# Ten blocks of experts: the second gate's logits of the first halves on three other engines

## The chip, the cores and the metric

The kernel runs on one core of a Trainium2 chip. The metric is the device time of one execution in microseconds (us). The engines are TensorE (PE; PEld is its weight load), VectorE (DVE), ScalarE (ACT), GpSimd (POOL) and SyncE (SP), each with an instruction queue of its own that it works off in order.

## What is computed

Attention with rotary positions over 4 x 8 heads, and then two layers of experts on the 2304 tokens of 512 numbers that come out. The cut shows the two layers.

```python
def _moe_ref(x, modality_id, w_gate, modality_bias, w1, w2):
    logits = x @ w_gate + modality_bias[modality_id]
    e_idx = np.argmax(logits, axis=1)
    ...                                    # gate_w: softmax probability of e_idx
    for e in range(E):                     # E = 8, w1 512 x 1024, w2 1024 x 512
        mask = e_idx == e
        h = np.maximum(x[mask] @ w1[e], 0.0)
        out[mask] = gate_w[mask, None] * (h @ w2[e])

def _moe2_ref(x, w_skip, w_gate, w1, w2):
    do_compute = x @ w_skip > 0
    out = x.copy()
    xc = x[do_compute]
    ...                                    # the same routing and experts on xc: y
    out[do_compute] = xc + y
```

With the inputs as they are drawn, 2171 tokens of the first layer go to one expert and 133 to another. Of its 2304 outputs 716 pass the skip test of the second layer: 487, 123, 93, 6, 4, 2 and 1 of them go to seven experts.

## The kernel before

The instructions of every engine are written in program order by hand, and no planner moves them. Attention fills about the first 350 us. In its tail the tokens are sorted by expert into a list in DRAM (list0), and the first block of the first expert layer is begun.

The first layer (moe1) works on blocks of 256 tokens of one expert. body(i) does block i: mm1 in four phases g, each followed by ACT's relu (m_hi) and DVE's remainder (m_lo), which together write hT as a high and a low part; then mm2 on the first 128 tokens (half 0) and on the second (half 1), each into a psum tile y of two buffers (psY). Between the two halves xt(i + 1) transposes the tokens of the next block. fetch gathers tokens from DRAM with POOL, seq_load loads an expert's weights with SP if the expert changes, and seq_split divides them into two parts on ACT and DVE (w1s, w2s). Blocks 0 to 8 are certain; from 9 on every body stands in a conditional of its own (nest, L1292). With these inputs there are ten blocks, and only the tenth has a new expert.

A half's epilogue, epi(i, t, stage), routes its tokens for the second layer while the blocks go on:

- stage 0: ACT scales y by the gate weight into x2; three small POOL operations prepare the token index.
- stage 1: PE turns x2 with four transposes into psT, ACT copies them out, and POOL scatters x2 to out in DRAM.
- stage 2: PE multiplies x2t by the nine columns of gate and skip weights (wg2s): the logits. DVE chooses the expert (one-hot oh) in eight small operations, ACT does the exponential.
- stage 3: PE counts with oh and with acc2, the running count of tokens per expert.
- stage 4: DVE works out the place in the second list and adds oh to acc2, and POOL scatters token and weight to list1.

Half 0's stages all lie in body(i), between the pieces of mm2 on half 1. Half 1's stages 1 to 4 lie behind the four phases of mm1 in body(i + 1), and those of the last block in the first block of the second layer.

The second layer (moe2) works on blocks of 128 tokens, ten here. It adds its result to out with a gather and a scatter per block. At the end of body(6) moe2_ahead takes the counts so far, picks the leading expert and fixes its first two blocks. Two pairs of raw weight tiles are used in turn: (raw1, raw2) and (raw1b, raw2b). Before the change the leading expert's weights are loaded into (raw1b, raw2b) in body(7) by ACT's queue, and those of the next expert into (raw1, raw2) in the last body by SP's.

Of the kernel before, what the change touches and what calls it, by code (L numbers as in the profile page):

```python
# [10 lines left out]
F32 = mybir.dt.float32  # L11
F32R = mybir.dt.float32r
BF16 = mybir.dt.bfloat16
I32 = mybir.dt.int32
AF = mybir.ActivationFunctionType
ALU = mybir.AluOpType
# [96 lines left out]
class Kernel:  # L113
# [6 lines left out]
    def run(self):  # L120
# [3 lines left out]
        self.lists = [dp.tile([NLIST, 2], F32, name=f"list{i}") for i in range(2)]  # L124
        self.ident = cp.tile([128, 128], F32, name="ident")
# [18 lines left out]
        with ExitStack() as s:  # L144
            self.wp = s.enter_context(tc.tile_pool(name="moe", bufs=1, reuse_waits="tile"))
            self.pp = s.enter_context(tc.tile_pool(name="mps", bufs=1, space=PSUM, reuse_waits="tile"))
            self.bank = lambda name: self.rot("ps" + name, [128, 512], psum=True)
            self.moe_tiles()
            self.moe1()
            self.moe2()  # L150
# [818 lines left out]
    def moe_tiles(self):  # L969
        wp = self.wp  # L970

        self.slots2 = [(self.raw1, self.raw2), (wp.tile([128, 4, F], F32, name="raw1b"), wp.tile([128, 8, DM], F32, name="raw2b"))]
        self.xh = [wp.tile([128, DM], F32, name=f"xh{i}") for i in range(2)] + [self.xh2]
        for t in self.xh:
            self.nc.gpsimd.memset(t, 0.0)
        self.xT2 = wp.tile([128, 2, 4, B2], F32R, name="xT2")
        self.slots["xT"] = [[self.xT0, wp.tile([128, 2, 4, B1], F32R, name="xT1")], 1]

# [132 lines left out]
    def moe1(self):  # L1111
# [12 lines left out]
        def xt(i, h):  # L1124
            if i >= q.n:
                return
            if h == 0:
                xts[i] = self.rot("xT", [128, 2, 4, B1], F32R)
            self.transposed(xts[i], self.xg[i % 2][:, h, :], h * 128)
# [19 lines left out]
        def epi(i, t, stage):  # L1149
            s = eps[i, t]  # L1150

            def tl_(name, shape, dt=F32):
                return self.rot("e_" + name, shape, dt)

            if stage == 0:

                l = q.ls[i][0]
                x2 = s["x2"] = self.rot(f"x2{t}", [128, DM], bufs=1)
                s["ti"] = self.rot(f"ti{t}", [128, 1], I32, bufs=1)
                s["v"] = self.rot(f"ev{t}", [128, 3], bufs=1)  # L1160
                s["tg"] = self.rot(f"tg{t}", [128, 2], bufs=1)
                nc.scalar.activation(x2, s["y"], AF.Copy, scale=l[:, t, 1:2])
                nc.gpsimd.tensor_copy(s["ti"], l[:, t, 0:1])
                nc.gpsimd.tensor_scalar(s["v"][:, 0:1], l[:, t, 0:1], float(N), None, op0=ALU.is_lt)
                nc.gpsimd.tensor_copy(s["tg"][:, 0:1], l[:, t, 0:1])
            elif stage == 1:
# [7 lines left out]
            elif stage == 2:  # L1174
                v = s["v"]
# [3 lines left out]
                lg, nm, d = tl_("lg", [128, E + 1]), tl_("nm", [128, 1]), tl_("d", [128, E])  # L1179
                nc.vector.tensor_copy(lg, pg[:, 0 : E + 1])  # L1180
# [7 lines left out]
                nc.vector.tensor_reduce(m8, t8, axis=AX.X, op=ALU.max)  # L1188
                nc.vector.tensor_scalar(v[:, 1:2], lg[:, E : E + 1], 0.0, v[:, 0:1], op0=ALU.is_gt, op1=ALU.mult)
# [3 lines left out]
            elif stage == 3:  # L1193
# [3 lines left out]
            else:  # L1197
                v, oh = s["v"], s["oh"]
                nc.vector.tensor_scalar(s["se"], s["se"], 1e-9, None, op0=ALU.add)
                nc.vector.reciprocal(s["tg"][:, 1:2], s["se"])  # L1200
# [7 lines left out]
                self.scatter(self.lists[1], si, s["tg"], E * CAP)  # L1208
# [5 lines left out]
        def body(i):  # L1214
            def load2(c):
                if i == sure - 2:
                    self.moe2_load(1, c)

            more = None if i < sure - 1 else self.n1 > i + 1 - NA1
            if more is not None:  # L1220

                with tc.If(self.n1_sp > i + 1 - NA1) as cmp:
                    pass
                with cmp.Else():
                    self.moe2_second()
# [9 lines left out]
            for g in range(4 if i else 0):  # L1235
                mm1(i, g)
                if i == sure - 2:
                    self.moe2_load(0, g)
                epi(i - 1, 1, g + 1)
# [9 lines left out]
            mm2(i, 0, range(0, 8))  # L1249
            epi(i, 0, 0)  # L1250
            xt(i + 1, 0)
            xt(i + 1, 1)
            mm2(i, 1, range(0, 2))
            epi(i, 0, 1)
            load2(0)
            mm2(i, 1, range(2, 4))
            epi(i, 0, 2)
# [12 lines left out]
            epi(i, 0, 3)  # L1270
            epi(i, 0, 4)
            epi(i, 1, 0)
# [23 lines left out]
        self.last = dict(eps[sure - 1, 1])  # L1296
        nest(sure)
        eps[-1, 1] = self.last
# [36 lines left out]

    def moe2_second(self):
        q = self.q2
        for i in range(2):
            self.load(q.slots[0][i], q.w[i], self.reg(self.e2, [ET.SP], E - 1))
# [4 lines left out]
    def moe2(self):  # L1344
# [14 lines left out]
        def body(i):  # L1359
# [30 lines left out]
            def last(stage):  # L1390

                if i == 0:
                    self.epi(-1, 1, stage)

            def split1(pieces):
                self.seq_split(q, i + 1, 0, pieces)
# [13 lines left out]

            if i == 0:
                split2(0, range(0, 4))
            mm1(0, range(0, 2))
            last(1)
# [5 lines left out]
            last(2)  # L1420
            mm1(1, range(0, 2))
            split1((0,))
            h_tr(0)
# [3 lines left out]
            last(3)  # L1427
# [5 lines left out]
            last(4)  # L1433
# [96 lines left out]
```

## Time and profile before

| | |
|---|---|
| median of 3 runs | 760.42 us (759.24 to 762.78) |
| the profiled execution | 761.6 us, its span 760.0 us |
| busy in the span: PE, PEld | 718.9 us (95%), 652.8 us (86%) |
| busy in the span: DVE, ACT, POOL | 504.1, 441.8, 360.6 us |
| granted TensorE clock, mean | 0.979 of full speed |

The span runs from the first to the last instruction of the profiled execution; times in the rows further down count from its start. A matmul's end is modelled, so the step from one row's start to the next is the safer length. Attention takes about 0 to 354 us, the first layer's blocks to 609 us, the second layer the rest.

### The profile page before, as it was taken

What the parts mean: (1) busy time and instruction counts of PE and PEld (TensorE: products, weight loads), DVE (VectorE), ACT (ScalarE), POOL (GpSimd) and SP (SyncE); (2) the same over time, 40 slices, a digit from 0 to 9 for tenths busy, and PEclk for the clock granted to TensorE, in tenths of its full rate; (3) what the DMA queues carried; (4) which work ended last, traced back from release to release, by engine and by line L of the source; (5) the groups of instructions that cost most, each with busy time, mean ns of one, the idle gap of its engine ahead of it and who ended that gap; (6) DMA issues with size and microseconds to landing.
All of it is one profiled execution on the core that took longest, in us unless ns stands there. A gap on an engine that the chain in (4) does not pass through costs nothing. (4 is left out here: it accounts for less than half of the span.)

```text
span 760.0 us, 15381 instructions
## 1 busy us (share of the span) xinstructions
PE 718.9 (95%) x4948; PEld 652.8 (86%) x4948; DVE 504.1 (66%) x1216; ACT 441.8 (58%) x940; POOL 360.6 (47%) x497
## 2 busy tenths in 40 slices
PE   6899999999999999979999999999999969999994
PEld 6799999999999999878889988998998858877773
DVE  6789999999999999972533323333437643489892
ACT  3788888888888888861222222222235432388781
POOL 7655576868686863344433231332435412132232
PEclk8899999999999999999999999999999989999997
DMA  5665555555656554560011101110785201679900
GB/s 139 134 156 135 136 132 140 129 129 135 161 115 145 137 118 87 136 191 1 14 58 46 54 31 41 43 42 29 235 293 171 95 6 40 245 251 332 335 26 20
DMA packets 75341, 92.30 MB, mean 121 GB/s; under 512 B 29582, under 2 KB 50318, under 8 KB 75232
## 3 DMA queue, kind: packets, MB, share of 16 engines
q1 hardware_dynamic: 66080, 73.75, 35.6%
q0 software_dynamic: 7200, 12.46, 5.3%
q10 hardware_dynamic: 1952, 4.85, 2.0%
q8 instruction: 43, 0.70, 0.4%
q14 instruction: 66, 0.54, 0.3%
HBM read 62.12 MB, written 12.95 MB: 99 GB/s over the span
## 5 line engine op out<-in xcount | busy, mean ns | idle before, releaser
L428 PE MATMUL S<-w1s 128*128 128x288 f32 x640 | 134.1, 323 | 4.0 <-ACT w1s L384 1.3
L1145 PE MATMUL psY<-w2s,hT 128*128 128x512 f32 x480 | 119.4, 397 | 0.0
L1096 PE MATMUL psM<-xT,w1s 128*128 128x256 f32 x864 | 110.9, 285 | 0.0
L428 PEld LDWEIGHTS S<-w1s 128*128 128x128 f32 x640 | 98.7, 192 | 8.8 <-ACT PP L445 1.7
L1096 PEld LDWEIGHTS psM<-xT,w1s 128*128 128x128 f32 x864 | 105.2, 189 | 0.6 <-issue 0.6
L1145 PEld LDWEIGHTS psY<-w2s,hT 128*128 128x128 f32 x480 | 87.2, 188 | 16.8
L445 ACT ACTIVATE PP<-S,nm 128x576 f32<-128x576 f32 x128 | 95.9, 749 | 6.5 <-DVE nm L441 4.4
L441 DVE TENSOR_REDUCE nm<-S 128x1 f32<-128x576 f32 x128 | 94.9, 751 | 3.8 <-PE S L428 3.7
L530 DVE TENSOR_TENSOR tl<-T,th 128x512 fp32r<-128x512 f32 x128 | 88.0, 688 | 12.6 <-ACT th L526 9.3
L523 PE MATMUL T<-ident,PP 128*128 128x128 f32 x512 | 94.3, 274 | 0.8 <-DVE w1s L397 0.4
L526 ACT CAST th<-T 128x512 fp32r<-128x512 f32 x128 | 75.2, 587 | 17.6 <-PE T L523 15.1
L557 PE MATMUL O<-th,vh 128*128 128x288 f32 x256 | 76.4, 331 | 0.9 <-ACT os L566 0.9
L1109 DVE SCALAR_TENSOR_TENSOR hT<-psM,hT 128x512 fp32r<-128x512 f32 x36 | 24.9, 691 | 65.8 <-ACT hT L1104 53.7
L1369 PE MATMUL psM<-w1s,xT 128*128 128x512 f32 x240 | 62.0, 406 | 6.3 <-DVEq L1292 6.3
L523 PEld LDWEIGHTS T<-ident,PP 128*128 128x128 f32 x512 | 63.9, 140 | 3.4 <-DVE tl L530 1.0
L1409 PE MATMUL psY<-w2s,hT 128*128 128x512 f32 x240 | 63.7, 403 | 2.7 <-DVE hT L1388 2.7
L557 PE MATMUL O<-tl,vh 128*128 128x288 f32 x256 | 64.4, 305 | 0.0
L1104 ACT ACTIVATE hT<-psM 128x512 fp32r<-128x512 f32 x36 | 21.5, 598 | 70.6 <-PE psM L1096 70.1
L960 POOL DMA_INDIRECT list<-tg,si x20 | 20.2, 1009 | 88.7 <-issue 56.6
L1369 PEld LDWEIGHTS psM<-w1s,xT 128*128 128x128 f32 x240 | 44.7, 192 | 16.5 <-issue 6.4
L328 POOL TENSOR_TENSOR mem_w<-qkn,mem_w 128x640 f32<-128x640 f32 x30 | 46.9, 1565 | 19.0 <-PE T L365 18.8
L1409 PEld LDWEIGHTS psY<-w2s,hT 128*128 128x128 f32 x240 | 42.9, 188 | 13.6 <-DVE hT L1388 5.1
(262 smaller groups left out, 1423.2 us busy)
## 6 DMA issues: line engine op xcount, KB each, us to landing
raw<-in_moe_w_dram SPq DMA_DIRECT2D x20, 512.0 KB
mem_w<-in_moe_w_dram SPq DMA_DIRECT2D x20, 512.0 KB
w1s<-w1s SPq DMA_DIRECT2D x30, 256.0 KB
raw1b<-in_moe_w_dram SPq DMA_DIRECT2D x12, 512.0 KB
raw2b<-in_moe_w_dram SPq DMA_DIRECT2D x12, 512.0 KB
w1s<-w1s SPq DMA_DIRECT2D x16, 288.0 KB
qkn<-in_q_dram SPq DMA_DIRECT2D x16, 256.0 KB
qkn<-in_k_dram SPq DMA_DIRECT2D x16, 256.0 KB
```

The costliest lines, as they stand in the source:

```text
L328: eng.tensor_tensor(r, x, tb[:, i, 0].unsqueeze(1).broadcast_to([128, 2, 5, D]), op=ALU.mult)
L428: yield nc.tensor.matmul(ps[:, hf, 0:288], s["wide"][:, o : o + 128], s["K"][h % 2][:, kk, hf * 288 : hf * 288 + 288], start=first and kk ...
L441: nc.vector.tensor_reduce(st[h // 2]["nm"][:, h % 2, c : c + 1], hs[h]["ps", c][:, :, 0:288], axis=AX.XY, op=ALU.max, negate=True)
L445: nc.scalar.activation(PP[:, c, h % 2 * S : h % 2 * S + S].rearrange("p (a b) -> p a b", a=2), hs[h]["ps", c][:, :, 0:288], AF.Exp, bias=s ...
L523: yield nc.tensor.transpose(ps[:, c * 128 : c * 128 + 128], PP[:, c, o : o + 128], ident)
L526: nc.scalar.copy(hs[h]["th"][:, j, 0:512], hs[h]["tp", j])
L530: nc.vector.tensor_tensor(s["tl"][:, j, 0:512], s["tp", j], s["th"][:, j, 0:512].bitcast(F32), op=ALU.subtract)
L557: yield nc.tensor.matmul(s["ot"][:, hf, 0:288], st[h // 2]["vh"][:, h % 2, j].rearrange("p s d -> p (s d)"), w[:, hf * 288 : hf * 288 + 28 ...
L1096: self.nc.tensor.matmul(ps[:, a], self.w1s[:, wi, dc, fs], x[:, xi, dc], start=(dc == 0 and wi + xi == 0), stop=(dc == 3 and wi == 1))
L1145: nc.tensor.matmul(ps, h[:, hi, f, t * 128 : t * 128 + 128], w2s[:, wi, f], start=(f == 0 and hi + wi == 0), stop=(f == 7 and hi == 1))
L1369: nc.tensor.matmul(ms[hf], x[:, xi, dc], w1s[:, wi, dc, hf * 512 : hf * 512 + 512], start=(dc == 0 and wi + xi == 0), stop=(dc == 3 and xi ...
L1409: nc.tensor.matmul(y, hT[:, hi, f], w2s[:, wi, f], start=(f == 0 and hi + wi == 0), stop=(f == 7 and hi == 1))
```

## The change

Half 0 of every block but the first gets its nine logits without PE. Its y or x2 is multiplied by a row of the gate weights that stands on all partitions, and summed along the row: three of the nine with a POOL product ("prod") and an ACT sum ("sums"), six with one DVE operation each that reads y from psum. gate_rows builds the nine rows before the first layer: four small transposes, a copy, a write to DRAM and nine reads that broadcast a row to all partitions. Eight of the rows lie in raw1b, which is why the weight tiles are paired anew and the loads of the second layer's first experts are moved: raw1 for the leading expert in the last body (moe2_last_loads), raw1b for the next one in the second layer's first block (moe2_second); the load of raw1b in body(7) is gone.

Half 1 of every block, and both halves of block 0, keep the transposes and matmuls ("turn", "gate"). The stages have names now, and half 0's logits, choice ("top"), "count" and "list" move from body(i) to the mm1 phases of body(i + 1); half 1's count and list move into the middle of mm2 there. The small index operations go from POOL to ACT and DVE ("meta"). The last block's epilogues, now of both halves, run in the second layer's first block, where h_tr(0) also moves ahead of split1((0,)) for every block.

```diff
...
-        self.slots2 = [(self.raw1, self.raw2), (wp.tile([128, 4, F], F32, name="raw1b"), wp.tile([128, 8, DM], F32, name="raw2b"))]
+        raw1b, raw2b = wp.tile([128, 4, F], F32, name="raw1b"), wp.tile([128, 8, DM], F32, name="raw2b")
+        self.slots2 = [(raw1b, self.raw2), (self.raw1, raw2b)]
+
+        self.gw = [raw1b.rearrange("p c f -> p (c f)")[:, e * DM : e * DM + DM] for e in range(E)]
+        self.gw.append(wp.tile([128, DM], F32, name="gw8"))
+        self.junk = wp.tile([128, DM], F32, name="junk")
...
+    def gate_rows(self):
+
+        nc = self.nc
+        ps = self.bank("G")
+        for c in range(4):
+            nc.tensor.transpose(ps[0 : E + 1, c * 128 : c * 128 + 128], self.wg2s[:, c], self.ident)
+        t = self.rot("x2t", [128, 4, 128])[0 : E + 1].rearrange("p c t -> p (c t)")
+        nc.scalar.copy(t, ps[0 : E + 1])
+        nc.sync.dma_start(self.wgt, t)
+        for e in range(E + 1):
+            nc.sync.dma_start(self.gw[e], self.wgt[e : e + 1].broadcast_to([128, DM]))
...
-            if stage == 0:
+            if stage == "meta":
 
                 l = q.ls[i][0]
-                x2 = s["x2"] = self.rot(f"x2{t}", [128, DM], bufs=1)
-                s["ti"] = self.rot(f"ti{t}", [128, 1], I32, bufs=1)
-                s["v"] = self.rot(f"ev{t}", [128, 3], bufs=1)
-                s["tg"] = self.rot(f"tg{t}", [128, 2], bufs=1)
-                nc.scalar.activation(x2, s["y"], AF.Copy, scale=l[:, t, 1:2])
-                nc.gpsimd.tensor_copy(s["ti"], l[:, t, 0:1])
-                nc.gpsimd.tensor_scalar(s["v"][:, 0:1], l[:, t, 0:1], float(N), None, op0=ALU.is_lt)
-                nc.gpsimd.tensor_copy(s["tg"][:, 0:1], l[:, t, 0:1])
-            elif stage == 1:
+                for name, w, dt in (("v", 3, F32), ("tg", 2, F32), ("lg", E + 1, F32), ("ti", 1, I32)):
+                    s[name] = self.rot(f"{name}_{t}", [128, w], dt, bufs=1)
+                nc.scalar.copy(s["tg"], l[:, t])
+                nc.scalar.copy(s["ti"], l[:, t, 0:1])
+            elif stage == "out":
+                s["x2"] = self.rot(f"x2{t}", [128, DM], bufs=1)
+                nc.scalar.activation(s["x2"], s["y"], AF.Copy, scale=s["tg"][:, 1:2])
+            elif stage == "prod":
+
+
+                s["prod"] = [self.rot("x2t", [128, 4, 128]).rearrange("p c t -> p (c t)") for _ in range(3)][0:2]
+                s["prod"].append(self.rot("prod", [128, DM], bufs=1))
+                for j, w in enumerate(s["prod"]):
+                    nc.gpsimd.tensor_tensor(w, s["x2"], self.gw[j], op=ALU.mult)
+                    if j == 0:
+                        self.scatter(self.out, s["ti"], s["x2"], N)
+            elif stage == "sums":
+                for j, w in enumerate(s["prod"]):
+                    nc.scalar.activation(w, w, AF.Copy, accum_out=s["lg"][:, j : j + 1])
+            elif isinstance(stage, tuple):
+
+                for e in stage:
+                    nc.vector.scalar_tensor_tensor(
+                        self.junk, s["y"], s["tg"][:, 1:2], self.gw[e], op0=ALU.mult, op1=ALU.mult, accum_out=s["lg"][:, e : e + 1]
+                    )
+            elif stage == "turn":
...
-            elif stage == 2:
-                v = s["v"]
+            elif stage == "gate":
                 pg = self.bank("G")
                 for dc in range(4):
                     nc.tensor.matmul(pg[:, 0 : E + 1], s["x2t"][:, dc], self.wg2s[:, dc], start=dc == 0, stop=dc == 3)
-                lg, nm, d = tl_("lg", [128, E + 1]), tl_("nm", [128, 1]), tl_("d", [128, E])
-                nc.vector.tensor_copy(lg, pg[:, 0 : E + 1])
+                nc.vector.tensor_copy(s["lg"], pg[:, 0 : E + 1])
+            elif stage == "top":
+                v = s["v"]
+                lg, nm, d = s["lg"], tl_("nm", [128, 1]), tl_("d", [128, E])
...
+                nc.vector.tensor_scalar(v[:, 0:1], s["tg"][:, 0:1], float(N), None, op0=ALU.is_lt)
...
-            elif stage == 3:
+            elif stage == "count":
...
-                nc.vector.reciprocal(s["tg"][:, 1:2], s["se"])
+                tg = self.rot("tgs", [128, 2], bufs=4)
+                nc.vector.reciprocal(tg[:, 1:2], s["se"])
+                nc.scalar.copy(tg[:, 0:1], s["tg"][:, 0:1])
...
-                self.scatter(self.lists[1], si, s["tg"], E * CAP)
+                self.scatter(self.lists[1], si, tg, E * CAP)
...
         def body(i):
+            def before(t, *stages):
+
+                for stage in stages if i else ():
+                    epi(i - 1, t, stage)
+
...
-                    self.moe2_second()
+                    self.moe2_last_loads()
+            before(1, "out")
...
             for g in range(4 if i else 0):
                 mm1(i, g)
-                if i == sure - 2:
-                    self.moe2_load(0, g)
-                epi(i - 1, 1, g + 1)
+
+                if i == 1:
+                    (
+                        lambda: before(0, "turn"),
+                        lambda: before(0, "gate", "top"),
+                        lambda: (before(0, "count", "list"), before(1, "turn")),
+                        lambda: before(1, "gate", "top"),
+                    )[g]()
+                else:
+                    (
+                        lambda: before(0, "sums", (3, 4, 5)),
+                        lambda: (before(0, (6, 7, 8)), before(1, "turn")),
+                        lambda: (before(0, "top"), before(1, "gate", "top")),
+                        lambda: before(0, "count", "list"),
+                    )[g]()
             if more is None:
                 self.seq_split(q, i + 1, 0)
             else:
@@ -1246,15 +1304,19 @@
                     self.split1(self.slots2[1][0])
             if i > 0:
                 self.seq_load(q, i + 2, 0)
-            mm2(i, 0, range(0, 8))
-            epi(i, 0, 0)
+            mm2(i, 0, range(0, 4))
+            before(1, "count", "list")
+            mm2(i, 0, range(4, 8))
+            epi(i, 0, "meta")
+            epi(i, 0, "out")
             xt(i + 1, 0)
             xt(i + 1, 1)
+            if i:
+                epi(i, 0, "prod")
             mm2(i, 1, range(0, 2))
-            epi(i, 0, 1)
+            epi(i, 1, "meta")
             load2(0)
             mm2(i, 1, range(2, 4))
-            epi(i, 0, 2)
...
-            epi(i, 0, 3)
-            epi(i, 0, 4)
-            epi(i, 1, 0)
             self.seq_split(q, i + 1, 1)
...
+    def moe2_last_loads(self):
+
+        q = self.q2
+        self.load(q.slots[1][0], q.w[0], self.reg(q.first["meta"][0:1, 0:1], [ET.SP], E - 1))
+        self.load(q.slots[0][1], q.w[1], self.reg(self.e2, [ET.SP], E - 1))
+
     def moe2_second(self):
         q = self.q2
-        for i in range(2):
-            self.load(q.slots[0][i], q.w[i], self.reg(self.e2, [ET.SP], E - 1))
+        self.load(q.slots[0][0], q.w[0], self.reg(self.e2, [ET.SP], E - 1))
 
...
+            last(1, "out")
+            last(0, "sums", (3, 4, 5), (6, 7, 8))
+            mm1(0, range(0, 1))
+            last(1, "turn")
+            if i == 0:
+                self.moe2_second()
+            mm1(0, range(1, 2))
+            last(0, "top")
             if i == 0:
                 split2(0, range(0, 4))
-            mm1(0, range(0, 2))
-            last(1)
             split2(i, range(4, 8))
             if i + 2 > NA2 + 1:
                 self.seq_load(q, i + 2, 1)
             mm1(0, range(2, 4))
             relu(0)
-            last(2)
+            last(0, "count", "list")
+            last(1, "gate", "top")
             mm1(1, range(0, 2))
+            h_tr(0)
             split1((0,))
-            h_tr(0)
             mm1(1, range(2, 4))
             split1((1,))
             relu(1)
-            last(3)
+            last(1, "count")
...
             mm2(range(0, 2))
-            last(4)
+            last(1, "list")
```

## Rows read from the trace of the kernel before

**Rows 1.** Windows of one block: length; busy PE, PEld, DVE, ACT, POOL; clock; DMA.
```profile
474.90:501.20 26.30, 26.30 (x183) 23.90 (x183) 8.61 (x38) 6.41 (x14) 8.35 (x14) 1.00 0.15 41
```

**Rows 2.** Waits of PE from 340 to 620 us: total, times, longest.
```profile
PE psM L1369 <- DVEq L1292: 6.3, 1, 6.3
...
PE psG L1195 <- DVE oh L1192: 1.7, 1, 1.7
PE psT L1170 <- DVE xT L1082: 1.3, 2, 1.0
PE psG L819 <- DVE acc L1204: 0.5, 1, 0.5
```

**Rows 3.** The chain that ended last: start, length, what.
```profile
667.45 6.02 DMA out_dram<-x,tok
```

**Rows 4.** Timeline of PE in block 6: start, length, what.
```profile
501.22 3.12 PE L1096 MATMUL psM<-xT,w1s 128*128 128x256 f32 x24
504.18 0.60 PE L1170 MATMUL psT<-ident,x 128*128 128x128 f32 x4
504.53 3.13 PE L1096 MATMUL psM<-xT,w1s 128*128 128x256 f32 x24
507.49 0.96 PE L1178 MATMUL psG<-wg2s,x2t 128*128 128x9 f32 x8
508.31 3.12 PE L1096 MATMUL psM<-xT,w1s 128*128 128x256 f32 x24
...
514.29 5.65 PE L1145 MATMUL psY<-w2s,hT 128*128 128x512 f32 x24
```

**Rows 5.** Instructions of one line: the gate matmuls, ns min/median/max.
```profile
L1178 PE MATMUL psG<-wg2s,x2t x160: 171/257/257, 364.2 to 621.3; 128*128 128x9 f32 x160
```

**Rows 6.** Costliest groups of the page: a POOL product.
```profile
L328 POOL TENSOR_TENSOR mem_w<-qkn,mem_w 128x640 f32<-128x640 f32 x30 | 46.9, 1565 | 19.0 <-PE T L365 18.8
```

**Rows 7.** Groups by form from 430 us: busy us, mean ns of one.
```profile
L994 ACT CAST w2s<-raw2b 128x512 fp32r<-128x512 f32 x32 | 17.1, 618 | 5.6 <-DVEq L1292 5.6
...
L1460 DVE SCALAR_TENSOR_TENSOR x<-psY,list,xh 128x512 f32<-128x512 f32 x10 | 7.5, 746 | 4.3 <-PE psY L1409 4.3
```

**Rows 8.** Instructions of one line: ACT's read of a sum.
```profile
L445 ACT ACTIVATION_READ_ACCUMULATOR PP<-S,nm x128: 190/202/243, 20.2 to 319.6; 128x1 f32 x128
```

**Rows 9.** Timeline of DVE in blocks 5 and 6.
```profile
498.49 0.17 DVE L1180 COPY e_lg<-psG 128x9 f32<-128x9 f32 x1 [2.36 <-PE psG L1178]
...
500.01 0.15 DVE L1199 TENSOR_SCALAR se<-se 128x1 f32<-128x1 f32 x1
...
505.06 0.69 DVE L1109 SCALAR_TENSOR_TENSOR hT<-psM,hT 128x512 fp32r<-128x512 f32 x1 [2.85 <-ACT hT L1104]
...
515.79 0.14 DVE L1199 TENSOR_SCALAR se<-se 128x1 f32<-128x1 f32 x1
...
516.68 0.16 DVE L1207 TENSOR_TENSOR si<-e_sf,ev 128x1 int32<-128x1 f32 x1
```

**Rows 10.** Timeline of DVE in the last block and behind the seam.
```profile
598.34 4.68 DVE L985 TENSOR_TENSOR w1s<-raw1b,w1s 128x1024 fp32r<-128x1024 f32 x4 [0.26 <-ACT w1s L981]
...
616.42 2.50 DVE L997 TENSOR_TENSOR w2s<-raw2b,w2s 128x512 fp32r<-128x512 f32 x4 [6.13 <-ACT w2s L994]
```

**Rows 11.** Timeline of PE at the seam of the two layers.
```profile
609.27 0.17 PE L1196 MATMUL psG<-acc,ones 128*128 128x8 bf16 x1
615.74 2.90 PE L1369 MATMUL psM<-w1s,xT 128*128 128x512 f32 x6 [6.30 <-DVEq L1292]
...
624.80 1.66 PE L1409 MATMUL psY<-w2s,hT 128*128 128x512 f32 x6
```

**Rows 12.** Timeline of POOL in block 6 and at the seam.
```profile
521.50 1.06 POOL L960 DMA_INDIRECT out_dram<-x,ti  x1 [2.60 <-DMA list<-tg,si]
...
611.06 0.99 POOL L960 DMA_INDIRECT list<-tg,si  x1 [7.10 <-issue]
```

**Rows 13.** DMA issues: times, median us from issue to landing.
```profile
list<-tg,si POOLq DMA_INDIRECT x20, 2.9
```

More of the change, by code (lines that the diff above doesn't have):

```diff
@@ L124, in run @@
         self.lists = [dp.tile([NLIST, 2], F32, name=f"list{i}") for i in range(2)]
+        self.wgt = dp.tile([E + 1, DM], F32, name="wgt")
         self.ident = cp.tile([128, 128], F32, name="ident")
@@ L148, in run @@
             self.moe_tiles()
+            self.gate_rows()
             self.moe1()
@@ L1294, in nest @@
                     nest(i + 1)
-        self.last = dict(eps[sure - 1, 1])
+        self.last = [dict(eps[sure - 1, t]) for t in range(2)]
         nest(sure)
-        eps[-1, 1] = self.last
+        for t in range(2):
+            eps[-1, t] = self.last[t]
     def moe2_ahead(self):
@@ L1388, in h_tr, with last @@
                 nc.vector.tensor_tensor(hT[:, 1, fs], p4, hT[:, 0, fs].bitcast(F32), op=ALU.subtract)
-            def last(stage):
-                if i == 0:
-                    self.epi(-1, 1, stage)
+            def last(t, *stages):
+                for stage in stages if i == 0 else ():
+                    self.epi(-1, t, stage)
             def split1(pieces):
```

## Prediction

> **What bounds the kernel now.** I read the busy times by stretch first, for the stage that the change touches, then what TensorE (PE) waits for there, then the chain of waits for what comes behind it. A block of the first expert layer takes 26.3 us, PE is busy in all of it at full clock, VectorE (DVE), ScalarE (ACT) and GpSimd (POOL) for 8.6, 6.4 and 8.4 us [rows 1]. So each microsecond taken off PE in these blocks is won, if the engines that take the work over are not late. PE's waits there are few: 1.7, 1.3 and 0.5 us, and 6.3 us at the seam, where the first layer's last conditional ends and the second layer begins [rows 2]. Behind the seam PE sets the pace until about 667 us; from then on the chain goes from scatter to gather through DRAM, as the first of its scatters shows, 6 us to land [rows 3], so work saved on PE there buys little, but the whole stretch starts when PE arrives: what is won before it is carried to the end.
>
> **What leaves PE.** A half's four transposes take 504.53 - 504.18 = 0.35 us, its gate matmuls 508.31 - 507.49 = 0.82 us [rows 4], 1.17 us in all. There are 160 gate matmuls, eight to a half [rows 5], so 20 halves, ten blocks. The second halves stay; of the ten first halves block 0's moves one block later, nine go: 9 x 1.17 = **10.5 us**. Three waits of rows 2 go with them. The 1.7 us is block 0's count waiting for a chain behind a busy POOL; that count is now a whole phase later. The 1.3 us, in two blocks, is the removed transposes waiting for their psum bank. The 0.5 us is the total for the second layer's first blocks, waiting for a list step that is now long done. Together **3.5 us**. The total then misses one half block; with the reference's inputs 487 of the 716 tokens that the second layer computes go to one expert, so the same expert leads and its two first blocks are full.
>
> **What is added to PE.** gate_rows: four transposes with nine output rows, once. Below: nothing; above: the four full transposes, 0.35 us. I take **0.4 us**. Its nine broadcasts go out on SP about 30 us before their first reader, with no SP load of the next blocks behind them.
>
> **Who takes the work over, in a block (t = 0 at its first matmul, 501.22).** POOL: three products of 512 elements; the nearest row is 1565 ns for 640 [rows 6], so 1.25 us each (bounds: 1.0 and 1.56). They start when ACT has written x2, at about t = 19.5, behind the list scatter, with the scatter to out between them: some 5 us, done near the block's end. The next block reads them at t = 3.8; their slack is about 4 us, which hides them. Behind them on POOL stand the next gathers, read 13 us later. POOL also loses three small operations per half.
>
> ACT: three sums at 0.62 us (the copy of 512 elements, [rows 7]) plus 0.2 us for the read of the sum [rows 8]: 2.5 us, from 3.8 to 6.3, where its next relu is due at 6.2. That hides it but for 0.1 us; psM has a second buffer.
>
> DVE: six multiply-and-sum operations. The nearest row has the same form without the sum, 746 ns [rows 7]; I take p = **0.75 us** each. The four matmul phases end at t = 2.96, 5.92, 9.23 and 13.0 (phases of 2.96 from rows 4, with the second half's turn and gate still between them); the hT step comes 0.88 us after a phase (505.06 - 504.18) and takes 0.69 [rows 9]. So hT 3.84 to 4.53; logits 3 to 5 until 6.78, hT due at 6.80; until 7.49; logits 6 to 8 until 9.74, hT due at 10.11; until 10.80; then the two choices of an expert, 1.5 us each (498.49 to 500.01, [rows 9]) and 0.2 us for a comparison that comes from POOL, until 14.2; the last hT until 14.9; the list step, 1.05 us (515.79 to 516.68 + 0.16), whose running count is ready after its fifth operation at 15.6. PE asks for that count after half of mm2, 13.07 + 2.8 = 15.9. It fits by 0.3 us. This is the step with the least slack: what is late there delays PE at once. p is free up to 0.815, and with that slack up to 0.865; above it each of the eight blocks 2 to 9 loses 6 x (p - 0.815) - 0.3.
>
> Bounds of p: 0.62, the pitch of a 512-element subtract [rows 10], and 0.95, if a sum costs DVE a second instruction as long as ACT's [rows 8]. At 0.95 the blocks lose 8 x 0.5 = 4.1 us. [...]
>
> **The seam.** PE's last matmul starts at 609.27, its next one at 615.74 [rows 11]. In between POOL issues the list scatter at 611.06 [rows 12], 1.0 us, which lands 2.9 us later [rows 13]; 0.8 us after that every engine is released. After the change POOL's last transfer is another: in the last block DVE ends list step 0 at t = 16.0, the w1 split of 4.7 us [rows 10] at 20.7, list step 1 at 21.7; then POOL's list scatter until 22.8. The scatter to out behind it waits for that one to land, as it does now [rows 12], so 25.7 to 26.7, and lands at 29.6; two products end at 29.2. Release near 30.4, with PE done at 26.3 - 1.2 = 25.1: a wait of 5.3 us for today's 6.4. The products may be slower than my 1.25 us, so I take **0** and hold -3.5 to +2.
>
> **The second layer's first block.** Here the cover is gone: out, sums, logits and choices of the last first half stand ahead of everything. Now mm2 begins 624.80 - 615.74 = 9.1 us after the seam [rows 11]. Afterwards DVE must do, in its order, six logits 4.5, choice 1.7, eight w2 pieces 2 x 2.5 [rows 10], list 1.05, choice 1.7, hT 0.7: 14.6 us, before the third matmul of mm2; so it starts at 14.1, **+5.0 us**. ACT comes to much the same: its relu stands behind eight w2 pieces, which stand behind the exponential of the choice. PE waits at its count, its h_tr and its mm2, in pieces. With p of 0.62 and 0.95: 4.2 and 6.2.
>
> **Other moves.** The loads: raw1b holds the gate rows, so the second layer's first w1 is loaded into raw1 as soon as the w1 split of the block before frees it (t = 20.7 there), some 18 us before its own split, instead of two blocks earlier; the second expert's w1 goes to the second layer's block 0, needed four blocks later. Hidden. POOL's list loads move with the first block. h_tr ahead of a w1 piece lets hT come up to 4.68 / 4 = 1.2 us earlier [rows 10] in the six later blocks with a new expert (seven experts have tokens): 0 to 7 us; I take 0, since there the DRAM chain is last.
>
> **Sum.** -10.5 - 3.5 + 0.4 + 0 + 5.0 = -8.6. The profiled execution took 761.6 us (span 760.0), so 753.0; it lies 1.2 above the median of the runs, 760.42, so **751.8**.
>
> **Rivals.**
> *The take-over fits, the first block of the second layer pays (forecast)*: 749.5 to 754.5. For it: the idle shares of rows 1. Chance 0.55.
> *The gain is eaten*: p at 0.95 gives back 4.1 + 1.2 us, and a seam 1 to 2 us longer through slow POOL products the rest: 757 to 759. For it: 0.3 us of slack in each block. Against: POOL has 18 us of idle time in a block. Chance 0.18, about a quarter of it still below 756.6.
> *Slower*: DVE's logits become the bound of each block. With all gain gone at p = 1.01 and 0.5% lost at 1.08; at twice my price, 1.5, each block loses 3.8 us and the first block 4.5, so 752 + 35 = 787. Against: the three-operand row stands at 746 ns with a PSUM input, as here. [...] Chance 0.11.
> *More than the sum*: the seam shrinks by its 3 us, or the earlier hT shortens the tail's blocks too: 747 to 749. For it: the six blocks. Against: rows 3. Chance 0.16.
>
> **Numbers.** Likeliest 751.8; the range 747.5 to 758.5 leaves out the slower case and little more. About 0.5% (3.8 us) can be told from no change. Faster: 0.55 + 0.16 + 0.04 = 0.75; within: 0.14; slower: 0.11.
>
> **What would show it.** 80 + 8 gate matmuls and 44 transposes of x2 instead of 160 and 80; blocks of about 25.1 us from block 2 on; no PE wait on acc2 above 0.3 us in them; DVE's logits at 0.75 us; a seam of 5 to 6.5 us; the second layer's mm2 starting 14 us after it; the same spacing of blocks behind it. Wrong if PE waits for the running count in every block, if the seam is much over 7 us, or if what PE wins is lost to the DRAM chain behind 667 us.

## The result and the profile after

The changed kernel takes **749.42 us** (749.02 to 752.11, 4 runs) where the kernel before took 761.6 in runs beside it (759.24 to 763.06, 4 runs): ratio 0.9843, interval 0.9816 to 0.987. 751.8 was forecast, with 747.5 to 758.5 as its range. Run again with the experiments, the same kernel gave 753.9 against 763.68, ratio 0.9862 (0.9827 to 0.9896), so the size is some 10 to 12 us. The profiled execution took 752.11 us, span 750.5, against a span of 760.0 before: -9.5, where the sum of the forecast was -8.6.

The total is close, its parts are not. Cut into stages on TensorE's timeline, profile against profile (us; attention is counted from PE's first instruction to the count ahead of the first block's mm2, so it holds the four transposes of gate_rows; the seam from PE's last mm2 matmul of the first layer to the first transposes for the second layer's second block):

| | before | after | forecast |
|---|---|---|---|
| attention | 353.0 | 353.4 (+0.4) | +0.4 |
| first layer | 254.5 | 243.4 (-11.1) | -14.0 |
| seam and the second layer's first block | 19.1 | 21.7 (+2.6) | +5.0 |
| the rest of the second layer | 131.8 | 130.5 (-1.4) | 0 |

First, one block, the window that answers to [rows 1] (its length; busy PE, PEld, DVE, ACT, POOL; clock; DMA):

```profile
492.68:517.66 24.98, 24.98 (x169) 22.55 (x168) 12.92 (x51) 8.27 (x25) 11.98 (x13) 1.00 0.13 43
```

26.3 us have become 25.0. PE is still busy in all of it at full clock, so it is still the bound; DVE has gone from 8.6 to 12.9, POOL from 8.4 to 12.0. What has left PE, from the groups of PE from 340 us on (against 160 gate matmuls in [rows 5]):

```profile
L1213 PE MATMUL psG<-wg2s,x2t 128*128 128x9 f32 x88 | 10.6, 248 | 0.0
L1206 PE MATMUL psT<-ident,x 128*128 128x128 f32 x44 | 7.1, 287 | 5.2 <-ACT x L1183 5.2
```

PE's waits from 340 us on (total, times, longest) show where the rest was lost; none of the three of [rows 2] that were to go is left at its place, and the 6.3 us of the seam are 0.7. Of the three waits for oh (the chosen expert, which the count reads) one lies in block 7, 0.67 us, one in block 8, 0.16, and the longest behind the seam:

```profile
PE psT L1206 <- ACT x L1183: 5.2, 1, 5.2
...
PE psM L1115 <- DVE hT L1128: 2.6, 1, 2.6
PE psG L1233 <- DVE oh L1230: 2.6, 3, 1.7
...
PE psM L1434 <- DVEq L1351: 0.7, 1, 0.7
```

PE's timeline in block 6 (as [rows 4]), at the count of block 7, in the first layer's last block, and behind the seam (as [rows 11]):

```profile
492.68 5.92 PE L1115 MATMUL psM<-xT,w1s 128*128 128x256 f32 x48
498.43 0.60 PE L1206 MATMUL psT<-ident,x 128*128 128x128 f32 x4
...
505.57 2.99 PE L1164 MATMUL psY<-w2s,hT 128*128 128x512 f32 x12
508.41 0.18 PE L1233 MATMUL psG<-oh,U 128*128 128x8 bf16 x1
...
531.50 0.17 PE L1233 MATMUL psG<-oh,U 128*128 128x8 bf16 x1 [0.67 <-DVE oh L1230]
...
578.21 4.62 PE L1115 MATMUL psM<-xT,w1s 128*128 128x256 f32 x24 [2.55 <-DVE hT L1128]
...
599.41 0.93 PE L1434 MATMUL psM<-w1s,xT 128*128 128x512 f32 x3 [0.72 <-DVEq L1351]
605.50 1.11 PE L1206 MATMUL psT<-ident,x 128*128 128x128 f32 x4 [5.16 <-ACT x L1183]
606.27 3.61 PE L1434 MATMUL psM<-w1s,xT 128*128 128x512 f32 x9
...
616.55 0.17 PE L1233 MATMUL psG<-oh,U 128*128 128x8 bf16 x1 [1.73 <-DVE oh L1230]
...
616.61 1.71 PE L1474 MATMUL psY<-w2s,hT 128*128 128x512 f32 x6
```

In block 6 two matmul phases run without a break in 5.75 us, where two phases of [rows 4] took 2 x 2.96, and the running count at 508.41 comes without a wait: the step that the forecast called the tightest holds there. In block 7 it doesn't: PE waits 0.67 us, where the forecast allowed 0.3. The two places where the change pays most are the last block and the seam. In the last block the 2.55 us of wait are not all: after it 24 matmuls take 4.46 us (578.21 to 582.67) instead of 2.96, at a granted clock of 0.62 in that window, where it was 1.00 in the phases ahead of the wait:

```profile
569.36:575.05 5.69, 5.69 (x49) 5.69 (x48) 5.69 (x5) 3.77 (x10) 5.00 (x5) 1.00 0.96 334
578.21:582.67 4.46, 4.46 (x25) 4.46 (x26) 4.32 (x12) 0.00 (x0) 1.79 (x2) 0.62 0.77 255
```

What DVE did ahead of that wait, beside POOL, from the timelines of both (the first row lies at the start of block 7, the last two behind the seam):

```profile
518.28 1.45 DVE L835 SCALAR_TENSOR_TENSOR f_t<-totc,f_mx,w 128x8 f32<-128x8 f32 x1
...
567.98 2.52 DVE L1016 TENSOR_TENSOR w2s<-mem_w,w2s 128x512 fp32r<-128x512 f32 x1
568.62 1.32 POOL L1190 TENSOR_TENSOR x2t<-x,raw1b 128x512 f32<-128x512 f32 x1
570.12 1.26 POOL L962 DMA_INDIRECT out_dram<-x,ti  x1 [0.17 <-issue]
570.42 4.09 DVE L1016 TENSOR_TENSOR w2s<-mem_w,w2s 128x512 fp32r<-128x512 f32 x2
571.39 1.31 POOL L1190 TENSOR_TENSOR x2t<-x,raw1b 128x512 f32<-128x512 f32 x1
572.64 1.31 POOL L1190 TENSOR_TENSOR prod<-x,raw1b 128x512 f32<-128x512 f32 x1
...
577.47 0.68 DVE L1128 SCALAR_TENSOR_TENSOR hT<-psM,hT 128x512 fp32r<-128x512 f32 x1
...
599.31 1.29 POOL L1190 TENSOR_TENSOR x2t<-x,raw1b 128x512 f32<-128x512 f32 x1
599.74 0.75 DVE L1199 SCALAR_TENSOR_TENSOR junk<-psY,tg,raw1b 128x512 f32<-128x512 f32 x1 [3.52 <-DVEq L1351]
```

The eight pieces of a w2 split cost DVE 0.61 us each without a product beside them (4.90 us for the eight in e6). Here the piece that meets the first product takes 2.52 us, and of the next two, 4.09 us together, one stands through both other products. The split ends 4.7 us late, and the hT that PE waits for is queued behind it. Behind the seam, what PE's 5.16 us hang on, from ACT's timeline:

```profile
604.76 0.69 ACT L1183 ACTIVATE x<-psY,tg 128x512 f32<-128x512 f32 x1 [10.50 <-DMA out_dram<-x,ti]
605.34 0.62 ACT L1195 ACTIVATE x2t<-x2t 128x512 f32<-128x512 f32 x1
605.86 0.19 ACT L1195 ACTIVATION_READ_ACCUMULATOR x2t<-x2t 128x1 f32 x1
605.96 0.62 ACT L1195 ACTIVATE x2t<-x2t 128x512 f32<-128x512 f32 x1
```

ACT writes the last half's rows into a buffer that a scatter of an earlier block has read, and stands until 604.76.

### The profile page after: what moved, and what is told of

Its sections match the earlier page's. It is cut to its first block, busy times and chain, and to the rows that moved or that the text cites. A ratio compares the mean times of both kernels' runs of the same rounds, so it can differ in the third digit from the quotient of the medians.

```text
span 750.5 us, 15355 instructions
## 1 busy us (share of the span) xinstructions
PE 709.6 (95%) x4844; PEld 643.2 (86%) x4844; DVE 548.4 (73%) x1335; ACT 458.2 (61%) x1046; POOL 376.3 (50%) x464
## 5 line engine op out<-in xcount | busy, mean ns | idle before, releaser
L1164 PE MATMUL psY<-w2s,hT 128*128 128x512 f32 x480 | 116.0, 396 | 0.0
L1164 PEld LDWEIGHTS psY<-w2s,hT 128*128 128x128 f32 x480 | 87.9, 188 | 17.3
L1474 PE MATMUL psY<-w2s,hT 128*128 128x512 f32 x240 | 62.2, 401 | 0.0
L962 POOL DMA_INDIRECT list<-tgs,si x20 | 21.5, 1076 | 80.0 <-issue 40.4
L1183 ACT ACTIVATE x<-psY,tg 128x512 f32<-128x512 f32 x20 | 13.8, 689 | 67.7 <-PE psY L1164 56.4
L1101 DVE TENSOR_TENSOR xT<-psT,xT 128x512 fp32r<-128x512 f32 x31 | 20.4, 686 | 44.2 <-ACT xT L1097 43.1
```

The source lines that it names most:

```text
L1164: nc.tensor.matmul(ps, h[:, hi, f, t * 128 : t * 128 + 128], w2s[:, wi, f], start=(f == 0 and hi + wi == 0), stop=(f == 7 and hi == 1))
L1474: nc.tensor.matmul(y, hT[:, hi, f], w2s[:, wi, f], start=(f == 0 and hi + wi == 0), stop=(f == 7 and hi == 1))
```

## The experiments

All were timed beside the kernel before. The trace tells their stages apart better than the times do: attention alone varies from 351.6 to 356.7 us between the profiled executions. The kernel before was timed anew for each group of experiments and took 760.9 to 764.0 us, so times of different groups are compared by their ratios.

**e1_order: the move of h_tr alone, in the kernel before.**

```
             mm1(1, range(0, 2))
-            split1((0,))
             h_tr(0)
+            split1((0,))
```

> The kernel before, with only the second layer's h_tr(0) moved ahead of the first w1 piece. Theory (part of the unforeseen gain is made in the second layer's later blocks by this move): PE's three waits of 0.9 us for DVE's hT vanish, 1 to 3 us in all, about 758 to 760 us where the kernel before has about 761. Rival (the chain of scatters and gathers through DRAM sets the tail, and the move hides behind it): within 1 us of the kernel before.

760.24 us against 763.97, ratio 0.9969 (0.9939 to 0.9998); the second layer behind its first block takes 129.9 us for 131.8. The order is worth about 2 us.

**e2_old_order: the changed kernel with the old order of these two lines.**

> The changed kernel, with h_tr(0) put back behind the first w1 piece. Theory (the move is worth 1 to 3 us): 750.5 to 752.5 us where the changed kernel has 749.4. Rival (hidden behind the DRAM chain): 748.5 to 750.5.

753.88 us, ratio 0.9871 (0.984 to 0.9902). The same stretch is 132.2 us where the changed kernel has 130.5, and PE again waits for DVE's hT five times, 4.4 us. So the 1.4 us that the rest of the second layer gained are this move's; the stages from the first layer on are 396.6 us long in e2 and 395.5 in the changed kernel, where the kernel before has 405.5.

**e3_tensor_all: the changed kernel's frame, every first half's logits on TensorE.**

```
-                if i == 1:
+                if True:
...
-                epi(i, 0, "prod")
...
-            last(0, "sums", (3, 4, 5), (6, 7, 8))
+            last(0, "turn")
...
-            last(0, "top")
+            last(0, "gate", "top")
```

> The changed kernel with its new order of stages and loads, but with all first halves' logits on TensorE (no products, sums or DVE logits). Theory (PE's work is what was saved, and the three engines gave part of it back: 4.1 us in the last block, where DVE's w2 split met POOL's products, and some 3 us in the second layer's first block): 9 x 1.17 = 10.5 us dearer, 7 us cheaper, so 752 to 754. Rival 1 (the new order made the gain, not the work taken off PE): 749 to 750, or less. Rival 2 (the last block's stall has nothing to do with POOL's products): 757 to 760.

762.86 us, ratio 0.9986 (0.996 to 1.0011): no change. The blocks go back to 26.2 us, but the last one takes 26.1 where the changed kernel has 29.2, with no wait for hT and a w2 split of 4.90 us; seam and first block are 19.3 us for 21.7. The take-over of the logits therefore wins about 1.3 us in each of eight blocks and loses 3 us in the last one and 2.4 at the seam. The time lies above every forecast of this run, and it doesn't fit the stages: from the first layer on e3 is 400.1 us long, 5.4 less than the kernel before and 4.6 more than the changed kernel. By the times nearly all of the change's gain is the take-over's, by the stages about half of it; these runs don't decide it.

**e4_dve_nine: all nine logits on VectorE, no products on GpSimd.**

```
-                        lambda: before(0, "sums", (3, 4, 5)),
-                        lambda: (before(0, (6, 7, 8)), before(1, "turn")),
+                        lambda: before(0, (0, 1, 2, 3, 4)),
+                        lambda: (before(0, (5, 6, 7, 8)), before(1, "turn")),
...
```

> The changed kernel with all nine logits of a first half on DVE, none on POOL and ACT (the scatter of the half's rows stays where it was). One logit takes DVE 0.80 us from start to start in the changed kernel. Theory (DVE's slack ends at 0.815 us for six logits, and with 0.3 us at the count): nine are as 1.2 us for six, each of eight blocks loses 6 x (1.2 - 0.815) - 0.3 = 2.0 us, 16 us in all, the second layer's first block 2.4 us; the last block wins its 4 us back: about 763. Rival (DVE has more slack than the sum said, since PE asks for less of it so early): under 755, and no PE wait above 0.5 us in blocks 2 to 6.

762.01 us, ratio 0.999 (0.9962 to 1.0018). Three more operations of 0.80 us put DVE over its slack: blocks of 26.2 us, and from the waits of PE, at the place that the prediction named as the tightest:

```profile
PE psG L1233 <- DVE oh L1230: 12.6, 10, 1.9
```

The loss is 1.26 us a block, not 2.0. The rival "DVE's logits become the bound" is thus real, three operations away.

**e5_change_again: the changed kernel, unedited, beside the next three.**

> The changed kernel itself, beside the three below. Theory and rival alike: a ratio of about 0.984 to the kernel before. It is here because the first four runs were few, and the kernel with all logits on TensorE came out 7 us slower by its times than its trace's stages say (4.5 us over the change): if its own ratio is nearer 0.988, the traces are right.

753.9 us, ratio 0.9862 (0.9827 to 0.9896). The waits of 5.0 us for ACT and of 1.8 for hT come again.

**e6_late_dve: nine logits on VectorE in the last two blocks and behind the seam, so that no product stands beside the last w2 split.**

```
...
-            if i:
+            if 0 < i < sure - 1:
                 epi(i, 0, "prod")
...
-            last(0, "sums", (3, 4, 5), (6, 7, 8))
+            last(0, (0, 1, 2, 3, 4), (5, 6, 7, 8))
```

> The changed kernel with the nine logits on DVE, and no products on POOL, for blocks from 8 on (the two first halves whose work lies beside the last w2 split and the seam). Theory (POOL's products and DVE's w2 split, with two SBUF inputs, held each other up: 9.6 us instead of 4.9): the split is back at 4.9 us, PE's wait of 2.6 us and the slower clock behind it go, 4 us, and the seam is 1 us shorter; three logits more cost the last block under 1.3 us: 3 to 5 us faster than the change. Rival (DVE's lateness in the last block comes from the order of its work, not from POOL): the split stays at 9 us, or PE waits as long for the added logits: within 1 us of the change.

753.89 us, ratio 0.9864 (0.9826 to 0.9902): no gain over e5. The mechanism is confirmed all the same: without the products the split is short again, beside POOL's scatter to out, which stays. The instructions of the split's line in the last block (ns, shortest, median, longest), e6 after the changed kernel's:

```profile
L1016 DVE TENSOR_TENSOR w2s<-mem_w,w2s x8: 678/679/3484, 568.0 to 576.8; 128x512 fp32r<-128x512 f32 x8
```

```profile
L1016 DVE TENSOR_TENSOR w2s<-mem_w,w2s x8: 682/684/685, 571.5 to 575.7; 128x512 fp32r<-128x512 f32 x8
```

The last block takes 26.2 us instead of 28.4 in e5. The nine logits give this back: in the block before (26.9 for 25.4), where PE now waits for DVE's hT and oh, and behind the seam (23.9 us for 21.7).

**e7_first_block_order: another order of the second layer's first block.**

```
...
+            mm1(0, range(0, 2))
...
             split2(i, range(4, 8))
...
+            last(1, "out")
             mm1(0, range(2, 4))
             relu(0)
...
+            last(0, "sums", (3, 4, 5), (6, 7, 8))
...
```

> The changed kernel with another order in the second layer's first block alone: w2 pieces ahead of the last epilogues on ACT and DVE, x2's scaling and turn behind mm1, list and choice of the last second half behind h_tr. Theory (PE's waits there, 5.2 us for ACT's x2 and 1.7 us for the choice, are a matter of order, since ACT stands behind POOL's reset of its DMA semaphores): mm2 starts about 12 us after the seam instead of 17.2, 4 to 5 us faster than the change. Rival (the lists come later, and the second layer's blocks 2 and 3 with them): the gain is given back before block 3, within 1 us of the change.

768.18 us, ratio 1.007, which says nothing about the order: by the code relu(0) writes over the second of the three products ahead of its sum here (both take the two buffers x2t in turn), so this half's rows go to other experts, and the second layer runs eleven blocks instead of ten. The reset that the theory speaks of is its author's reading: at the end of the conditional POOL's queue has one instruction INC_SWDGE_SEM, 2.09 us long in the changed kernel, and no run shows that it resets anything.

**e8_late_tensor: the last two blocks' logits and those behind the seam on TensorE, in e7's order.**

```
-                if i == 1:
+                if i == 1 or i >= sure:
...
-            if i:
+            if 0 < i < sure - 1:
                 epi(i, 0, "prod")
...
+            mm1(0, range(0, 2))
+            last(0, "turn")
...
+            last(1, "out")
...
```

> The changed kernel with TensorE's logits for first halves from block 8 on, as before the change, and the other order of the second layer's first block. Theory (both costs of the change lie at the end of the first layer and vanish with it): 4 us from the last block less 1.3 us of PE work, 6 us from the first block of the second layer: 741 to 743. Rival (it only moves the waits behind the seam into later blocks, where the DRAM chain is last): 746 to 749.

752.6 us, ratio 0.9847 (0.981 to 0.9885). The last block is 26.2 us without a wait, but seam and first block only went from 21.7 to 21.3, so neither forecast holds: PE still waits 3.3 us for ACT's write. ACT's timeline shows that this is another wait than the changed kernel's:

```profile
603.45 4.25 ACT L1013 CAST w2s<-raw2b 128x512 fp32r<-128x512 f32 x8
607.61 0.68 ACT L1183 ACTIVATE x<-psY,tg 128x512 f32<-128x512 f32 x1
```

ACT isn't idle ahead of the write: in this order the eight w2 pieces stand in front of it. So e8 doesn't tell what held ACT in the changed kernel; e9 to e11 take away the buffer that it writes there.

**e9_own_x2: the changed kernel, the last second half's rows in a buffer of their own.**

```
-                s["x2"] = self.rot(f"x2{t}", [128, DM], bufs=1)
+                s["x2"] = self.rot("x2own" if i < 0 else f"x2{t}", [128, DM], bufs=1)
```

> The changed kernel; the last second half's rows are written to a buffer of their own that no transfer has read. Theory A: behind the seam ScalarE stood because the buffer that it writes was read by a transfer of GpSimd, and the wait for it ends only when GpSimd has closed its queue at the end of the conditional (604.55). Then the write begins right behind the seam, TensorE's wait of 5.16 us for it falls below 1.5 us, and the first block of the second layer takes 17 to 19 us instead of 20.6; whole time 746.5 to 748.5 where the changed kernel has 749.4. Theory B (rival): ScalarE stands for something else that ends there, such as the products of GpSimd that it reads next or the end of the conditional itself: the write stays at 5 us behind the seam and the time is that of the changed kernel.

746.42 us (745.49 to 748.47), ratio 0.982 (0.9795 to 0.9845), which overlaps the changed kernel's; the stage decides: seam and first block 18.8 us for 21.7. From the timelines of ACT and PE:

```profile
596.02 0.69 ACT L1183 ACTIVATE x2own<-psY,tg 128x512 f32<-128x512 f32 x1 [4.63 <-PEq L1351]
...
596.59 0.94 PE L1434 MATMUL psM<-w1s,xT 128*128 128x512 f32 x3 [0.77 <-DVEq L1351]
597.37 0.60 PE L1206 MATMUL psT<-ident,x2own 128*128 128x128 f32 x4
597.72 2.35 PE L1434 MATMUL psM<-w1s,xT 128*128 128x512 f32 x9
603.28 0.17 PE L1233 MATMUL psG<-oh,U 128*128 128x8 bf16 x1 [3.21 <-DVE oh L1230]
...
610.85 1.71 PE L1474 MATMUL psY<-w2s,hT 128*128 128x512 f32 x6
```

ACT writes right behind the seam and PE's turn no longer waits: theory A. What PE waits for next, 3.21 us, is DVE's chain of six logits and a choice, as the prediction had it.

**e10_late_tensor_own: e9, with the logits from the ninth block on left on TensorE.** Edits as in e9, and the first two of e8; behind the seam "turn" and "gate" as in e3.

> As e9, and the logits of the blocks from the ninth on stay on TensorE as before the change, in the changed kernel's order of the first block. Theory A: no product of GpSimd stands beside the last w2 split, so the last block takes 26.2 us instead of 29.2; behind the seam no sums, no six logits and no wait for a transfer are left: first block 14 to 17 us instead of 20.6. The two together give back 6 to 9 us less 1.4 us for the extra work on TensorE in two blocks: 741 to 745 us. Theory B: the first block is set by VectorE's and ScalarE's w2 splits and the two choices behind them, so that it stays near 20 us: 746.5 to 748.5 us, won in the last block alone.

**743.99 us** (742.07 to 745.49), ratio 0.9776 (0.9752 to 0.98), whose interval lies below those of the changed kernel (0.9816 to 0.987 and 0.9827 to 0.9896): it beats the kernel before and the changed one. The last block takes 26.2 us, seam and first block 17.5. PE's waits from 420 us on are now small:

```profile
PE psT L1449 <- ACT x2t L1444: 4.4, 7, 1.2
PE psG L1233 <- DVE oh L1230: 2.8, 3, 1.7
PE psT L1206 <- ACT x2own L1183: 0.9, 1, 0.9
```

**e11_late_order_own: e10 in e8's order, with the write first.**

> As e10, with the other order of the first block (e8's), the second half's rows written first. Theory A: the 3.27 us that TensorE waited in e8 for ScalarE's write go, and with them its lower clock in the four matmul stretches behind it: first block 15 to 17 us where e8 had 20.0, whole time 4 us below e8's 752.6. Theory B: the wait moves to the choice of an expert or to the w2 pieces: 19 to 20 us, and a time within 1 us of e8's.

747.8 us (747.02 to 749.96), ratio 0.9835 (0.9812 to 0.9858). Seam and first block take 19.8 us for e8's 21.3: the wait for ACT's write is gone, since the write now stands ahead of the w2 pieces and has its own buffer (this run doesn't tell the two apart), but DVE's choices come later in this order than in e10's. That lies between the two theories, and the two ratios, each with its own runs of the kernel before, hardly differ.

## Why the prediction came out

**What leaves PE: right, a little too small.** 88 and 44 for 160 and 80, as forecast; a block loses 1.3 to 1.5 us instead of 1.17, since two phases that now follow each other directly save a further 0.17.

**The take-over in a block: right.** The groups by form of the three engines:

```profile
L1199 DVE SCALAR_TENSOR_TENSOR junk<-psY,tg,raw1b 128x512 f32<-128x512 f32 x40 | 29.9, 747 | 4.4 <-DVEq L1351 3.5
L1199 DVE DVE_READ_ACCUMULATOR junk<-psY,tg,raw1b 128x1 f32 x40 | 3.3, 83 | 0.0
L1190 POOL TENSOR_TENSOR x2t<-x,raw1b 128x512 f32<-128x512 f32 x14 | 18.3, 1311 | 0.2
L1195 ACT ACTIVATE x2t<-x2t 128x512 f32<-128x512 f32 x16 | 9.9, 624 | 0.0
L1195 ACT ACTIVATION_READ_ACCUMULATOR x2t<-x2t 128x1 f32 x16 | 3.1, 194 | 0.0
```

A logit steps by 0.80 us, below the 0.815 that was free; the product takes 1.31 for 1.25; ACT's sums step by 0.61, their read hidden, for the 0.82 forecast. The trace records each logit as two instructions on DVE, 40 and 40 here; the second one takes 83 ns, not the 0.2 us of the upper bound. Twice the price, 1.5 us a logit, as the slower case has it, was the author's estimate; no run shows it.

**The first layer as a whole: 2.9 us less than forecast, by a step that was missing.** The prediction asked whether POOL's products come in time, and not what runs on DVE meanwhile. In the last block it is a w2 split, and this costs 4.3 us against the blocks ahead (29.2 to 24.9): 2.55 of wait and 1.5 of lower clock behind it make up nearly all of it. e3, e4, e6 and e8 have no product there and a split of 4.9 us. With it the stretches add up, from one block's transposes of xg to the next block's: -1.8 in the first, -1.4 in each of five, -1.0 in each of two (in which PE waits 0.67 and 0.16 us for oh), +1.7 in the last and -1.9 behind it: -11.1. The prediction's terms, laid on the same stretches, are -1.7, five times -1.17, -1.7, -1.17, -2.2 and -1.4: -14.0 without gate_rows. So the last block is 3.9 us worse than forecast and block 7 is 0.7 worse, and the others together are 1.7 better. In block 7 DVE has moe2_ahead's small operations ahead of its first hT, the one of 1.45 us at 518.28 among them; from 523.30 on it works without a break up to the oh that PE waits for.

**The seam: the step failed.** The prediction let PE go when POOL's last transfer has landed, and took 0. PE in fact goes with DVE (its releaser in both rows), 3.6 us after the list scatter of DVE's last step is issued (595.81 to 599.41; 4.7 in [rows 11, 12]), and that step now lies 2.5 us ahead of PE's last mm2 matmul (598.30) instead of 2.1 behind it (609.00). The scatter, which lands 3.0 us after its issue, in POOL's timeline, and the instructions with which DVE's queue leaves the conditional:

```profile
595.81 0.98 POOL L962 DMA_INDIRECT list<-tgs,si  x1 [4.30 <-DVE xT L1101]
```

```profile
L1351 DVEq EVENT_SEMAPHORE  x2: 21/21/21, 599.2 to 599.4; - x2
```

POOL's later transfer and products don't hold PE: that scatter is issued at 598.28 and lands at 601.61, and the last product ends at 601.83. That DVE stands for just the list scatter is read from distances, but these repeat: in all eight traces that record this scatter's landing (the changed kernel, e2, e5 and e7 to e11), DVE's queue goes on 0.40 to 0.50 us after it. (The landing of [rows 13] counts from the start of the issue, so the prediction counted the issue's 1.0 us twice; that is not what failed.) So PE's wait fell by 5.6 us, beyond the held -3.5. But ACT did not go with PE. The scatter that last read its buffer, issued at 583.90, had landed 2.1 us later; yet ACT goes on only when POOL's queue has closed the conditional, with an instruction from 602.4 on, 2.09 us long. From the instructions of that line:

```profile
L1351 POOLq INC_SWDGE_SEM  x1: 2086/2086/2086, 602.4 to 602.4; - x1
```

ACT's write starts 0.3 us behind it, and in e2 to e6 0.26 to 0.28 us behind it. e9 shows that the wait hangs on the buffer; that it ends with this instruction is read from the distance. That wait was in no sum. mm2 starts 17.2 us after the seam instead of 14.1; with the wait removed (e9) it starts 14.3 us after it, and DVE works from 596.91 to 611.31 without a break, 14.4 us for the 14.6 of the prediction's chain. So the working of the chain of logits, choices and pieces was right, and two errors, -5.6 for PE and +3.1 for ACT, left +2.6 in place of +5.0.

**Behind it: h_tr.** 0 was taken out of "0 to 7"; e1 and e2 show 1.7 to 2.0.

**The sum.** First layer 2.9 short, seam and first block 2.4 better, tail 1.4 better: the total came within 1 us partly by luck, because a missing loss and a missing gain were of one size. The median lies where the forecast case (749.5 to 754.5) meets the case "more than the sum" (747 to 749), and of the latter both mechanisms were there, the shorter seam and the earlier hT.

**Left open.** e3's median lies 9 us above e2's, the stages of their profiles only 3.5 apart; e3's profiled execution (758.4) was the shortest of its ten. And in e8, e10 and e11 the stretch after the last matmul is 2.3 us longer than in the changed kernel. In each of them POOL's queue then stands 2.3 us between two of its semaphore instructions (736.54 to 738.86 in e10); why, no run shows.

## What to carry to other kernels

When work is handed to another engine, look at what the engines beside it run at that moment, not only at whether the taker has idle time: DVE's pieces of the w2 split stood beside POOL's products here, and the last block took 4.3 us more, 2.55 of it PE's wait for the hT that was queued behind them. At the end of a conditional look for buffers that a transfer has read: one buffer of its own for the first write behind the seam was worth 3 us of its stage here. And put the new work only into the stages with cover: leaving it out of the last two blocks and the seam, together with that buffer, gave the best version.

## What the hardware showed that was not expected

The three DVE operations of this trace that read from SBUF alone, two or more tiles each, and met a product of POOL did not slow down beside it; by their ends they stood. Two pieces of the w2 split took 2.52 and 3.48 us for 0.68, 1.8 and 2.8 us more, beside one product of 1.32 and two of 1.31, which are no longer than the others (1.29 to 1.33 us for those into x2t). Each of the two pieces ends 0.56 us behind the product's end, about the 0.61 us that a piece takes alone. e2, e5, e7 and e9 give the same two pieces (2.50 to 2.52 and 3.47 to 3.49 us); beside POOL's scatter alone (e6, 572.41 to 573.61) the pieces keep their 0.68. And the tiny operation at 518.28 on eight columns, 227 ns before the change, took 1.45 us beside the product at 518.41. The logit at 599.74, one of whose two large inputs lies in PSUM, takes its usual 0.75 us beside the product of 599.31. The piece recorded as started first (567.98, ahead of the product at 568.62) is the long one, so the recorded starts don't tell which of two such operations will stand. What DVE and POOL share there, no run shows.

Also not expected: behind 2.55 us of wait the 24 matmuls took 1.5 us more (4.46 for 2.96), at a granted clock of 0.62; in e9 the 3.21 us of wait are followed by five microseconds at 0.50. That the wait brings the lower clock is read from this order alone:

```profile
603.30:608.40 5.10, 5.10 (x20) 4.41 (x20) 5.03 (x12) 3.74 (x9) 0.67 (x1) 0.50 0.58 212
```
